# A fused attention and mixer kernel: the last batch's up products by seven products of quarters, joined score chunks for pairs 4 to 6, later transposes, key copies on VectorE

## The chip, the cores and the metric

One core of a Trainium2 chip. The metric is the device time of one execution in microseconds (us); less is better. The core has five engines that work side by side: TensorE (PE, with PEld for its weight loads), VectorE (DVE), ScalarE (ACT), GpSimd (POOL) and SyncE (SP, which issues most DMAs here). Each engine runs its own instructions in order and waits on semaphores for the others.

## What is computed

Attention with a local window, global keys and a linear bias, then a mixer: a low-rank product over the tokens and a two-layer product over the channels, each added to its input.

```python
# q, k, v: [4, 8, 768, 64]; n_global = 8, n_local = 96
scores = q @ k.T / 8                       # per batch and head
keep = (pos_k < 8) | ((rel >= 0) & (rel < 96))
a = softmax(where(keep, scores - slope[h] * dist, -1e9))
x = (a @ v).transpose(0, 2, 1, 3).reshape(4, 768, 512)
h = x.transpose(0, 2, 1) @ U @ V           # U: [768, 32], V: [32, 768]
u = x + h.transpose(0, 2, 1)
out = u + maximum(u @ w_ch1, 0) @ w_ch2    # [512, 2048], [2048, 512]
```

`u @ w_ch1` with its maximum is called the up products here, the product with `w_ch2` the down products.

## The kernel before

**Work and its order.** Heads are taken in pairs: 16 pairs, four to a batch (`NP = 4`). The order of all instructions is the order in which the Python code issues them (a manual schedule, L153); no planner moves them. Pairs 0 to 3 run in the loop at L778. Pairs 4 to 15 and two rounds more run in the loop at L835. One round `i` of it does the scores and exponentials of pair `i`, the product with v of pair `i - 1`, the low-rank part of pair `i - 1`, and, between these, a number of units of the channel products of earlier batches: `fill(n)` (L743) issues `n` units, and the tuple at L838 says how many stand at each place. `unit()` (L757) takes an up unit from `ups_q` or a down unit from `downs_q`, in turn as long as both are there and an up group is less than two groups ahead. `queue_ff(b)` (L604) puts the units of batch `b` into the queues; it is called for batch 3 in round 17. What is left after the loop runs at L937.

**Scores.** A pair's scores have 1408 columns for each of two heads (`W`), in three chunks of 512, 512 and 384. `scores` (L348) issues a chunk's matmuls (64 rows of the array each, one head in each half). Chunks 0 and 1 go to the two banks of the tile "sc" (one buffer, L82), and so does chunk 2 in `st_S(i, 2)`. `s_dve` (L401) then lets VectorE scale a chunk, add the bias and write it to the tile "sp" (one buffer). In `st_S12` (L422), used for pairs 7 to 15 (`joined`, L866), chunk 2 follows chunk 1 at once and goes to two of the three "th" banks (L90); VectorE reads chunk 2 first and chunk 1 later. `st_E` (L428) is the exponential on ScalarE, one instruction per head. `st_V` (L435) is the product with v, into the bank "ob" (one buffer).

**Transposes.** For pairs 1 to 7 `st_T` (L243) turns q and k by twelve transposes on TensorE into two "th" banks; ScalarE copies q out (L276), VectorE k (L277). `st_KA` (L287) makes a copy of the keys in which the global keys stand at the head of each block: two copies, on GpSimd for pairs 5 to 7 (L280). Pairs 8 to 15 are transposed by DMA.

**Up units.** A group is 256 tokens, three groups to a batch. An up unit (`mk_up`, L643) is eight matmuls with 256 columns (tokens) into one "th" bank, the weights `w1_16` in place, and one Relu of ScalarE that empties the bank into `htr` (L658):

```python
for k in range(2):
    jt = 2 * jp + k
    for dc in range(done, NDC):
        nc.tensor.matmul(hps[:, k * FT:(k + 1) * FT],
                         w1_16[:, dc, jt * P:(jt + 1) * P], uT[:, dc, ts], ...)
```

Eight units make a group. `uT` is the transposed `u`; the part of each pair comes by a DMA transpose (`st_X`, L520).

**Down units.** For batches 1 to 3 the down products of a group are done by seven products of quarters (`mk_product`, L697; a form of Strassen's method by Winograd): x1, y1, x2, y2, x3, y3, x4, eight matmuls with 256 columns each into one of two banks; after each, VectorE adds the bank to `x_sb` (L712). Their sums of weights (t1 to t4) are made once, their sums of `htr` (s1 to s4) per group by VectorE (`queue_sums`, L622; `queue_sum`, L568), each issued at the place in the order where `fill` takes it from the queue.

Of the kernel before, what the change touches and what calls it, by code (L numbers as in the profile page):

```python
# [11 lines left out]
FP32 = mybir.dt.float32  # L12
FP16 = mybir.dt.float16
# [3 lines left out]
ALU = mybir.AluOpType  # L17
# [3 lines left out]
def kernel(  # L21
# [44 lines left out]
    HJ = NJC // 2  # L66
    HD = DM // 2
    WG = tuple((b, g) for b in range(1, B) for g in range(NFG))

    cst = ctx.enter_context(tc.tile_pool(name="cst", bufs=1))  # L70
    wbig = ctx.enter_context(tc.tile_pool(name="wbig", bufs=1))
# [8 lines left out]
    def ps_sc():  # L80

        return psum.tile([P, 2, 512], FP32, name="sc", tag="sc", bufs=1)  # L82
# [160 lines left out]
    def st_T(i):  # L243
        stq, stk = cast.pop(i)
        qT = kp.tile([P, S], FP16, name="qT", tag="qT")
        kT = kp.tile([P, S], FP16, name="kT", tag="kT")
        kA = kp.tile([P, NSB - 1, P], FP16, name="kA", tag="kA")
        tps = []
        for st in (stq, stk):

            tp = ps_th("tp", FP16, S)
            tps.append(tp.rearrange("d (n p) -> d p n", n=NSB))
            for n in range(NSB):
                nc.tensor.matmul(  # L254
                    tp[:, n * P:(n + 1) * P], st[:, n].rearrange("s h d -> s (h d)"), ident16,
                    is_transpose=True, start=(n == 0), stop=(n == NSB - 1),
                )
# [161 lines left out]
    def st_S(i, c):  # L419
        s_dve(i, scores(i, c, False))  # L420
# [178 lines left out]
    def weight(w, j):  # L599
        return tw[w][:, j] if w != "t3" else tw[w][j // 2][:, j % 2]  # L600

    first_ups = []

    def queue_ff(b):  # L604
        for g in range(NFG):
            queue_group(b, g)
        if b == 0:
            for c in range(4):
                for made in first_ups:
                    ups_q.extend(made[2 * c:2 * c + 2])  # L610

    def queue_group(b, g):
# [101 lines left out]
                    store(*what)  # L714
            return go

        if b:
            for at in range(NJC // 2):
                ups_q.append((mk_up(at), (b, g)))
        else:  # L720
            first_ups.append([(mk_up(at), (b, g)) for at in range(NJC // 2)])
# [10 lines left out]
        else:  # L732
# [2 lines left out]
                order.sort(key=lambda u: max(1, u[1]))  # L735
            for u in order:
                downs_q.append((mk_down(*u), (b, g)))

    ahead, held, kept = [0], [True], deque()

# [94 lines left out]
    for i in range(NP, NPAIR + 2):  # L835
# [139 lines left out]
```

## Time and profile before

| what | value |
|---|---|
| median of 3 runs | 228.5 us (228.26 to 228.91) |
| the profiled execution | 227.39 us |
| its span, first to last instruction | 225.6 us |
| busy: TensorE / weight loads / VectorE / ScalarE / GpSimd | 218.0 / 171.4 / 156.1 / 126.2 / 73.8 us |
| granted TensorE clock | 1.000 |
| up matmuls (L653) | 756, 95.0 us busy |
| down matmuls of products (L707) | 504 |

The page of the profile gives busy times per engine, the span in 40 slices (each digit a busy share in tenths), the chain of work that ended last (followed back from the last instruction to what released it, step by step), and groups of equal instructions. A group's row reads: line, engine, operation, output<-input, shapes, count | busy us, mean ns of one | idle us just before them and what ended it. A row of the timeline reads: start us, length us, engine, line, operation, shapes, count, and in brackets the idle time before and what ended it. Matmuls overlap in the array: a matmul's recorded length is longer than the distance to the next one's start, and only starts tell the rate.

### The profile page before, as it was taken

To read this page: it belongs to the slowest core of one execution; us is meant where nothing else is said; L and a number is where in the kernel's file an instruction comes from. 1 tells how busy PE (TensorE), PEld (TensorE's weight loads), DVE (VectorE), ACT (ScalarE), POOL (GpSimd) and SP (SyncE) were. 2 spreads that over 40 slices of the span, in tenths; PEclk is the share of its full clock that TensorE was granted. 3 is DMA by queue.
4 is the path that set the end of the run, shared out by engine and by line. 5 is a ranking of instruction groups with operands and counts; after the bars stand their busy time and mean duration, and the time that the engine had idled before them with its cause. 6 is when DMAs were issued, how large, how long until landed. Compare 5 with 4: busy or idle time off the path is not lost.

```text
span 225.6 us, 5876 instructions
## 1 busy us (share of the span) xinstructions
PE 218.0 (97%) x2420; PEld 171.4 (76%) x2420; DVE 156.1 (69%) x320; ACT 126.2 (56%) x197; POOL 73.8 (33%) x124
## 2 busy tenths in 40 slices
PE   7989999999999999999999999999999999999993
PEld 2456678788754547888888888888998888888882
DVE  3798665749488988598989698898575534435552
ACT  6777867685806254967584947473733433333320
POOL 6498828297547412231313132313111000000000
PEclk9999999999999999999999999999999999999999
DMA  6999999969998999998989994960622102020112
GB/s 193 316 287 257 283 219 238 324 120 172 195 169 177 195 230 232 209 255 200 195 224 220 252 229 116 140 170 12 102 59 77 53 1 96 0 93 3 46 49 94
DMA packets 86563, 36.68 MB, mean 163 GB/s; under 512 B 74152, under 2 KB 83592, under 8 KB 86536
## 3 DMA queue, kind: packets, MB, share of 16 engines
q1 hardware_dynamic: 81480, 32.01, 60.6%
q0 software_dynamic: 5056, 4.29, 12.7%
q8 instruction: 19, 0.31, 0.6%
q14 instruction: 8, 0.07, 0.1%
HBM read 27.46 MB, written 6.29 MB: 150 GB/s over the span
## 4 chain that ended last, share of the span: by engine, by line
PE 85%; DVE 8%; ACT 2%; DMA 2%; issue 0%; SPq 0%
PE hps L653 35%; PE cx L707 13%; PE cy L707 10%; PE cps L688 9%; PE sc L367 3%; PE tp L254 3%; PE ob L448 2%; PE ob L444 2%; PE sc L533 2%; DMA kst<-in_k_dram 2%; PE sc L374 2%; ACT ep L431 1%; DVE x_sb L467 1%; DVE sp L413 1%; DVE x_sb L712 1%; DVE kA L290 1%
## 5 line engine op out<-in xcount | busy, mean ns | idle before, releaser
L653 PE MATMUL hps<-uT,w 128*128 128x256 f16 x756 | 95.0, 273 | 0.0
L658 ACT ACTIVATE htr<-hps 128x512 f16<-128x512 f32 x96 | 56.6, 600 | 55.7 <-PE hps L653 55.7
L653 PEld LDWEIGHTS <-w 128*128 128x128 f16 x756 | 71.2, 98 | 9.1
L413 DVE SCALAR_TENSOR_TENSOR sp<-sc,relcat 128x1024 f32<-128x1024 f32 (+1 forms) x27 | 32.1, 1189 | 8.5 <-PE sc L374 4.1
L431 ACT ACTIVATE ep<-sp 128x1408 f16<-128x1408 f32 x24 | 33.2, 1384 | 0.0
L470 POOL CAST x<-x_sb 128x384 f16<-128x384 f32 x27 | 14.2, 527 | 48.3 <-DVE x_sb L467 44.8
L707 PEld LDWEIGHTS <-htr 128*128 128x128 f16 x288 | 27.2, 98 | 3.1
L712 DVE TENSOR_TENSOR x_sb<-cx,x_sb 128x256 f32<-128x256 f32 x36 | 15.2, 421 | 19.0 <-PE cx L707 18.3
L688 PE MATMUL cps<-w,htr 128*128 128x512 f16 x96 | 23.9, 379 | 0.0
L707 PEld LDWEIGHTS <-s 128*128 128x128 f16 x216 | 20.4, 98 | 2.7
L541 POOL CAST x<-x_sb 128x768 f16<-128x768 f32 x12 | 10.2, 851 | 31.2 <-DVE x_sb L538 31.2
L712 DVE TENSOR_TENSOR x_sb<-cy,x_sb 128x256 f32<-128x256 f32 x27 | 11.4, 422 | 12.6 <-PE cy L707 12.4
L467 DVE TENSOR_TENSOR x_sb<-ob,rcp 128x384 f32<-128x384 f32 x30 | 16.7, 558 | 1.1
L367 PEld LDWEIGHTS <-kT 64*128 64x128 f16 x192 | 8.6, 93 | 11.5 <-issue 10.1
L448 PE MATMUL ob<-v,ep 128*128 128x65 f16 x192 | 16.4, 194 | 0.0
L367 PE MATMUL sc<-qT,kT 64*128 64x128 f16 x192 | 15.7, 220 | 0.0
L448 PEld LDWEIGHTS <-ep 128*128 128x128 f16 x192 | 13.8, 98 | 2.0 <-issue 0.3
L688 PEld LDWEIGHTS <-htr 128*128 128x128 f16 x96 | 8.4, 98 | 8.3
L444 PE MATMUL ob<-vA,ep 128*128 128x65 f16 x160 | 14.3, 194 | 0.2 <-DVE vA L317 0.2
L142 POOL CAST v<-vst 128x768 f16<-128x768 f32 x16 | 13.5, 842 | 3.0 <-DMA vst<-in_v_dram 3.0
L538 DVE TENSOR_TENSOR x_sb<-sc,x_sb 128x768 f32<-128x768 f32 x12 | 11.5, 958 | 4.0 <-PE sc L533 3.9
L374 PE MATMUL sc<-qT,kA 64*128 64x128 f16 x160 | 13.3, 217 | 0.8 <-DVE kA L290 0.6
(111 smaller groups left out, 319.2 us busy)
## 6 DMA issues: line engine op xcount, KB each, us to landing
qst<-in_q_dram SPq DMA_DIRECT2D x16, 384.0 KB, 4.0
kst<-in_k_dram SPq DMA_DIRECT2D x16, 384.0 KB, 5.7
vst<-in_v_dram SPq DMA_DIRECT2D x16, 384.0 KB, 4.0
out_dram<-x_sb SPq DMA_DIRECT2D x23, 256.0 KB, 2.0
w<-in_moe_w_ch_dram POOLq DMA_DIRECT2D x8, 512.0 KB, 8.1
vA<-v SPq DMA_DIRECT2D x8, 152.3 KB, 3.3
out_dram<-x_sb SPq DMA_DIRECT2D x2, 128.0 KB
uT<-x SPq DMA_TRANSPOSE x12, 4.4
```

The lines of the kernel that those rows point to most:

```text
L367: nc.tensor.matmul(scs[hi][:, o:o + P], kT[r, kb * P:(kb + 1) * P], qT[r, kb * P:(kb + 1) * P], start=(o == 0 and not on_pe), stop=(o + P ...
L374: nc.tensor.matmul(scs[hi][:, o + P:o + 2 * P], kA[r, kb], qT[r, (kb + 1) * P:(kb + 2) * P], start=False, stop=(o + 2 * P == tot),)
L413: nc.vector.scalar_tensor_tensor(out=sps[i][:, :, c0:c0 + tot], in0=both[:, :, 0:tot], scalar=qk_scale / slope[2 * (i % NP)], in1=relfs[c0 ...
L431: nc.scalar.activation(eps[i][:, hi], sps[i][:, hi], AF.Exp, scale=slope[2 * (i % NP)])
L444: nc.tensor.matmul(ob[:, qi], ep[:, OF[qi - 1]:OF[qi - 1] + P], vA[:, qi - 1, hi], start=True, stop=False,)
L448: nc.tensor.matmul(ob[:, qi], ep[:, DG[qi]:DG[qi] + P], vt[:, qi, hi], start=(qi == 0), stop=True,)
L467: nc.vector.tensor_tensor(xo, ob[:, :, 0:D], rb, ALU.mult)
L653: nc.tensor.matmul(hps[:, k * FT:(k + 1) * FT], w1_16[:, dc, jt * P:(jt + 1) * P], uT[:, dc, ts], start=(dc == 0 and k == 0), stop=(dc == ...
L658: nc.scalar.activation(cell["htr"][:, 2 * jp:2 * jp + 2].rearrange("p j t -> p (j t)"), hps, AF.Relu)
L688: nc.tensor.matmul(cps, htr[:, jc, t * P:(t + 1) * P], w2_16[:, jc], start=(b > 0 and jc == 0), stop=(jc == NJC - 1),)
L707: nc.tensor.matmul(ps, cell[a][:, j], weight(w, j), start=(first and j == 0), stop=(done is not None and j == HJ - 1), skip_group_check=True,)
L712: nc.vector.tensor_tensor(x_sb[:, n, cs], ps, x_sb[:, n, cs], ALU.add)
```

## The change

- **Up products of batch 3.** The 24 up units are replaced by seven products of quarters for each group and each of two halves of the hidden channels (`st`): 42 steps of eight matmuls with 128 columns. The four tiles of weight sums per half (`up_sums`) are made by VectorE from round 15 on, in buffers that the loads of q and k and "sp" no longer need. Four token differences per group (`token_sums`) are made by VectorE between the rows. Products 1, 6, 7 and 4 pile up in one "th" bank, 5 and 3 in a bank of "sc", 2 in "ob". ScalarE copies the banks after 2, 3 and 5 to SBUF; VectorE adds those copies to the "th" bank after 1, 6 and 7 and writes `htr`; ScalarE applies the Relu, in place for these, from the bank for 4. Two or three steps make a row, which takes the place of an up unit in `ups_q`; the steps of a group's end are mixed with the first of the next.
- **Pairs 4 to 6** use `st_S12`, as pairs 7 to 15 do.
- **The transposes of pairs 5 to 7** (`st_T(i + 1)`) move from behind `st_V(i - 1, 0)` to the place where chunk 2 of pairs 4 to 6 was; the load of the last quarter of `w1` now is issued on GpSimd's queue ahead of them instead of behind.
- **The key copies of pairs 5 to 7** go to VectorE.

```diff
         if i > NP:
-            st_KA(i, nc.gpsimd)
+            st_KA(i, nc.vector)
@@
+    def up_sums():
+        made = {0: [], 1: []}
+        room = scp.tile([P, 2 * W], FP32, name="uw", tag="sp", bufs=1)
+        later_set = room[:, 0:16 * P].bitcast(FP16).rearrange("p (x d n) -> p x d n", x=4, d=2)
+        part["p2"] = room[:, 16 * P:20 * P]
+        for st in range(2):
+            js = [slice(h * DFF // 2 + st * 4 * P, h * DFF // 2 + (st + 1) * 4 * P) for h in range(2)]
+            w = {f"a{h + 1}{d + 1}": w1_16[:, 2 * d:2 * d + 2, js[h]] for h in range(2) for d in range(2)}
...
+            for name, a, b_, op in (
+                ("s1", "a21", "a22", ALU.add), ("s2", "s1", "a11", ALU.subtract),
+                ("s4", "a12", "s2", ALU.subtract), ("s3", "a11", "a21", ALU.subtract),
+            ):
+                made[st].append((f"tw{name}", st, w[name], w[a], w[b_], op))
+    def queue_up_sums(st):
+        if st == 0:
+            uw["sums"] = up_sums()
+        for k, x in enumerate(uw["sums"][st][0:3 if st else 4]):
+            queue_sum(*x, wait=k)
+    def token_sums(g, t):
...
+        return [(f"tu{g}{n}", 0, q_[n], q_[a], q_[b_], ALU.subtract) for n, a, b_ in (
+            ("t1", "b12", "b11"), ("t2", "b22", "t1"), ("t3", "b22", "b12"), ("t4", "b21", "t2")
+        )]
+    def queue_products(b, cells, sums):
+        yy = ps_sc()
...
+        def add(g, st, h, t, x, y):
+            to = out_of(g, st, h, t)
+            x, y = (z.rearrange("p (j t) -> p j t", j=4) for z in (x, y))
+            nc.vector.tensor_tensor(to, x, y, ALU.add)
+            nc.scalar.activation(to, to, AF.Relu)
+        def step(g, st, k):
...
+            bank, a, t = {
+                1: ("x", "a11", "b11"), 2: ("z", "a12", "b21"), 3: ("y", "s4", "b22"),
+                4: ("x", "a22", "t4"), 5: ("y", "s1", "t1"), 6: ("x", "s2", "t2"),
+                7: ("x", "s3", "t3"),
+            }[k]
...
+            for j in range(4):
+                for dc in range(2):
+                    nc.tensor.matmul(
+                        ps[:, j * P:(j + 1) * P], uw[st][a][:, dc, j * P:(j + 1) * P],
+                        turns[g][t][:, dc], start=(k in (1, 2, 5) and j == 0 and dc == 0),
+                        stop=(k in (2, 3, 4) and j == 3 and dc == 1), skip_group_check=True,
+                    )
+            early = g == WU[0][1] and st == 0
+            if k in (2, 3, 5):
...
+                nc.scalar.copy(part["p5", st] if k == 5 else part[f"p{k}"], ps)
+            if k == 1:
+                add(g, st, 0, 0, ps, part["p2"])
+            elif k == (3 if early else 6):
+                add(g, st, 0, 1, made[at, "x"], part["p3"])
+            elif k == 7:
+                add(g, st, 1, 1, ps, part["p5", st])
+            elif k == 4:
+                nc.scalar.activation(
+                    out_of(g, st, 1, 0), ps.rearrange("p (j t) -> p j t", j=4), AF.Relu
+                )
+                sums[g](st)
+        rows = []
+        for _, g in WU:
+            first = g == WU[0][1]
+            if first:
+                rows += [[(g, 0, 2), (g, 0, 1)], [(g, 0, 5), (g, 0, 6)], [(g, 0, 3), (g, 1, 5)]]
+            else:
+                rows[-2].insert(0, (g, 0, 5))
+                rows[-1].insert(0, (g, 0, 2))
+                rows += [[(g, 0, 1), (g, 0, 3)], [(g, 0, 6), (g, 1, 5)]]
+            rows += [[(g, 1, 2), (g, 0, 7)], [(g, 1, 1), (g, 0, 4)], [(g, 1, 3), (g, 1, 6)],
+                     [(g, 1, 7)], [(g, 1, 4)]]
+        between = {k: uw["sums"][1][x:x + 1] for k, x in ((4, 3),)}
+        for k, (_, g) in enumerate(WU):
+            for at, x in ((7 * k - 2, (0, 1)), (7 * k, (2,)), (7 * k + 1, (3,))):
+                if k == 0:
+                    at += 2
+                between.setdefault(at, []).extend(todo[g][y] for y in x)
...
@@ the loop over pairs 4 to 15
         if i == NP:
             load_w1(2)
-        if i + 1 < NPE:
-            st_T(i + 1)
-        if i == NP:
             load_w1(3)
         fill(next(units))
-        joined = live and i >= NPE - 1
-        if joined:
+        if live:
             mid = st_S12(i)
-        elif live:
-            st_S(i, 1)
         fill(next(units), quiet=i > NP + 1 and (i - 2) % NP == NP - 1)
         if NP < i <= NPAIR:
             st_V(i - 1, 1)
-        if joined:
+        if live:
             s_dve(i, mid)
...
         fill(next(units))
-        if live and not joined:
-            st_S(i, 2)
+        if i + 1 < NPE:
+            st_T(i + 1)
         fill(next(units))
...
+        if NPAIR - 1 <= i:
+            queue_up_sums(i - NPAIR + 1)
```

A row's entry is (group, half, product); `between` names the rows after which VectorE makes token differences.

More of the change, by code (lines that the diff above doesn't have):

```diff
@@ L68 @@
     WG = tuple((b, g) for b in range(1, B) for g in range(NFG))
+    WU = tuple((B - 1, g) for g in range(NFG))
     cst = ctx.enter_context(tc.tile_pool(name="cst", bufs=1))
@@ new lines, in queue_products, with out_of, mk_row, go @@
+    def queue_products(b, cells, sums):
+        yy = ps_sc()
+        made = {}
+        rooms = [scp.tile([P, W], FP32, name="tu", tag="ep") for _ in range(2)]
+        places = [rooms[g // 2][:, g % 2 * 4 * P:(g % 2 + 1) * 4 * P] for g in range(NFG)]
+        part["p3"] = rooms[1][:, 4 * P:8 * P]
+        todo = {
+            g: token_sums(g, places[g].bitcast(FP16).rearrange("p (x d n) -> p x d n", x=4, d=2))
+            for _, g in WU
+        }
+        def out_of(g, st, h, t):
+            return cells[g]["htr"][:, h * HJ + 4 * st:h * HJ + 4 * st + 4, t * P:(t + 1) * P]
+        def add(g, st, h, t, x, y):
[4 more added lines that the diff above has]
+        def step(g, st, k):
+            at = (g, st)
+            if "htr" not in cells[g]:
+                cells[g]["htr"] = ffp.tile([P, NJC, FT], FP16, name="htr", tag="htr", bufs=3)
+            if k == 1:
+                made[at, "x"] = ps_th("hps")
+            elif k == 2:
+                made[at, "z"] = ps_ob()
+            elif k == 5:
+                made[at, "y"] = yy[:, st]
+            bank, a, t = {
[3 more added lines that the diff above has]
+            }[k]
+            if a[0] == "s":
+                need((f"tw{a}", st))
+            if t[0] == "t":
+                need((f"tu{g}{t}", 0))
+            ps = made[at, bank]
+            for j in range(4):
[7 more added lines that the diff above has]
+            if k in (2, 3, 5):
+                if k == 5:
+                    part["p5", st] = stp.tile([P, 4 * P], FP32, name="p5", tag="vst", bufs=2)
+                nc.scalar.copy(part["p5", st] if k == 5 else part[f"p{k}"], ps)
+            if k == 1:
+                add(g, st, 0, 0, ps, part["p2"])
[13 more added lines that the diff above has]
+                rows += [[(g, 0, 2), (g, 0, 1)], [(g, 0, 5), (g, 0, 6)], [(g, 0, 3), (g, 1, 5)]]
+            else:
+                rows[-2].insert(0, (g, 0, 5))
[9 more added lines that the diff above has]
+                between.setdefault(at, []).extend(todo[g][y] for y in x)
+        def mk_row(n):
+            def go():
+                for s_ in rows[n]:
+                    step(*s_)
+                for x in between.pop(n, ()):
+                    nc.vector.tensor_tensor(*x[2:])
+                    have.add(x[:2])
+            return go
+        for n, row in enumerate(rows):
+            ups_q.append((mk_row(n), (b, row[-1][0])))
@@ L602 @@
     first_ups = []
     def queue_ff(b):
+        cells, sums = {}, {}
         for g in range(NFG):
-            queue_group(b, g)
+            cells[g], sums[g] = queue_group(b, g)
+        if (b, 0) in WU:
+            queue_products(b, cells, sums)
         if b == 0:
@@ L715, in mk_product @@
             return go
-        if b:
+        if (b, g) in WU:
+            pass
+        elif b:
             for at in range(NJC // 2):
```

15 lines of the change are left out of this document (added).

## Prediction

> **What bounds the kernel now.** I read the page's busy times first, then its slices, then the chain of work that ended last.
>
> ```profile
> PE 218.0 (97%) x2420; PEld 171.4 (76%) x2420; DVE 156.1 (69%) x320; ACT 126.2 (56%) x197; POOL 73.8 (33%) x124
> ...
> PE   7989999999999999999999999999999999999993
> ...
> DVE  3798665749488988598989698898575534435552
> ACT  6777867685806254967584947473733433333320
> POOL 6498828297547412231313132313111000000000
> ```
>
> TensorE (PE) is full from the third slice on. The other engines matter only where TensorE waits for them. The chain says the same: 85% of the span is TensorE, 35% of it the up products.
>
> ```profile
> PE 85%; DVE 8%; ACT 2%; DMA 2%; issue 0%; SPq 0%
> ```
>
> Two stretches are touched. The first is 31 to 60 us (pairs 4 to 6). There is one pair of it below, in the timeline of TensorE (start, length, line):
>
> ```profile
> 39.79 0.23 PE L367 MATMUL sc<-qT,kT 64*128 64x128 f16 x2
> ...
> 40.47 0.50 PE L254 MATMUL tp<-ident,q 128*128 128x128 f16 x6
> 41.05 0.49 PE L254 MATMUL tp<-ident,k 128*128 128x128 f16 x6
> 41.53 1.03 PE L653 MATMUL hps<-uT,w 128*128 128x256 f16 x8
> 42.50 0.23 PE L367 MATMUL sc<-qT,kT 64*128 64x128 f16 x2
> ```
>
> Lengths include a pipeline tail of 0.17 us; starts count. Eight 256-wide matmuls from 41.53 last 0.873 (0.109 each, as everywhere), so they end at 42.40. The scores begin 0.10 later, and leaving the scores costs another 0.09 (last start 55.26 plus 0.06, next matmul 55.41). That is the price of each visit to the scores. The k transposes should have begun at 40.47 + 6 x 0.056 = 40.81 and began 0.24 late, the next unit 0.14 late: both waited for ScalarE to empty one of the three "th" banks behind two Exps, as ScalarE's timeline shows:
>
> ```profile
> 39.12 1.39 ACT L431 ACTIVATE ep<-sp 128x1408 f16<-128x1408 f32 x1
> 40.39 1.09 ACT L658 ACTIVATE htr<-hps 128x512 f16<-128x512 f32 x2
> ```
>
> (The second Relu ends at 41.48, TensorE starts at 41.53: 0.05 from release to matmul.)
>
> The second stretch is the last batch's up products, from 177.09 to the end of TensorE at 221.63. Busy time by window:
>
> ```profile
> 187.00:200.00 13.00, 13.00 (x121) 11.66 (x120) 5.59 (x13) 4.69 (x9) 0.00 (x0) 1.00 0.11 42
> ```
>
> TensorE has no gap; VectorE (third number) is at 5.6 of 13, ScalarE at 4.7, the granted clock is 1.00. The durations that I use are these (last numbers: busy, mean ns), with the latency from the timeline: a product ends at 190.19, VectorE's add starts at 190.39, so 0.20.
>
> ```profile
> L658 ACT ACTIVATE htr<-hps 128x512 f16<-128x512 f32 x96 | 56.6, 600 | 55.7 <-PE hps L653 55.7
> ...
> L693 DVE TENSOR_TENSOR x_sb<-cps,x_sb 128x512 f32<-128x512 f32 x6 | 4.1, 681 | 0.0
> ```
>
> ```profile
> 190.39 0.42 DVE L712 TENSOR_TENSOR x_sb<-cx,x_sb 128x256 f32<-128x256 f32 x1 [2.19 <-PE cx L707]
> 190.73 0.41 DVE L571 TENSOR_TENSOR s<-htr 128x512 f16<-128x512 f16 x1
> ```
>
> ```profile
> 69.99 0.49 PE L533 MATMUL sc<-tmp,v16w 128*128 128x128 f16 x6
> 70.33 0.38 PE L688 MATMUL cps<-w,htr 128*128 128x512 f16 x1
> ```
>
> The next VectorE instruction starts 0.08 before the last one's end (190.39, 190.73), when it depends on nothing; on ScalarE it is 0.12. Six 128-wide matmuls take 0.34: 0.056 each, their weight loads included.
>
> **The change, part by part.**
>
> **1. Products.** Out go 24 units of 8 matmuls, 192 x 0.1092 = 20.97. In come 42 steps (7 products, 2 halves, 3 groups) of 8 matmuls of 128 columns: 336 x 0.056 = 18.82. Gain 2.15 on TensorE. The trace has such matmuls only in runs of 6 to 12; here they come in runs of 8 to 24, each with a new weight. The weight-load row is 98 ns long, but 65-wide matmuls with a load each start every 0.031 (11 in 0.35, from 40.12), so loads keep up. The Trainium skill speaks against this: "TensorE: Matmul & The Clock Gate", section "Back-to-back issue gap", gives about 81 ns per matmul for a sustained stream of 128 columns with weight loads. By it the 336 would take 27.2 and lose 6.2 where I count a gain of 2.15; the row of 0.056 differs from it, in short runs.
>
> **2. What the products add on VectorE and ScalarE.** Per group: six adds of a bank and a stored part (512 wide, float32 in: 0.68, from L693), four token differences (256 wide, half words: 0.29, between L271's 0.17 for 24 columns and L571's 0.42 for 512), eight copies or Relus from PSUM and six Relus in place (0.60 each, from L658 and L391's 0.594). VectorE rises from 5.6 to 5.6 + 6 x 0.68 + 4 x 0.29 = 10.8 of about 12.4, ScalarE to 14 x 0.60 = 8.4. Neither is the bound by sum. But TensorE must now wait for adds inside a chain: products 1, 6, 7 and 4 pile up in one bank, and VectorE reads it between them. A step is 0.448, a down product 0.874. I went through the instruction order with these figures:
> - *Handing over to the next group* (3 times, the start included). Step 3 and then step 6 end; a down product (0.87) follows; then step 5 of the next group needs t1. The copy of step 3's bank ends 0.20 + 0.60 after step 3, which is 0.35 after step 6; the add of step 6 waits for it and starts at 0.39; VectorE takes t1 behind it at 0.99; t1 is there at 0.99 + 0.29 + 0.05 = 1.33. TensorE comes at 0.87 and waits **0.46**. Three times 1.38.
> - *The double row* between groups 0 and 1, the only place without a down product between: step 7, step 2 (0.45), step 4. Counted from step 6's end again, VectorE does t1, t2, s1, the add of the down product, s2, and begins the add of step 7 at 2.43; it is through at 3.11 + 0.05, TensorE is there at 2.67: **0.49**.
> - *The last two rows* hold one step each. Step 7 comes 0.87 after step 6 but its bank is free at 0.39 + 0.68 + 0.05 = 1.12: **0.25**; step 4 likewise waits behind two sums and an add: **0.29**.
> - Elsewhere the slack is positive, least 0.16 (step 1 to step 6: 1.32 between them; the add needs 0.20 + 0.22 of queue + 0.68 + 0.05).
>
> Sum of waits 2.41, less 2.15: the tail **loses 0.26**. The add's bounds are the rows 0.43 (L571, half words) and 0.96 (L538, 768 wide): with 0.43 the waits sum to 0.88 (tail -1.27), with 0.96 to 5.7 (+3.6). I take 0.68, whose width and types are nearest. t1 at 0.17 or 0.42 moves the tail by -0.37 or +0.64.
>
> **3. Eight weight sums** (1024 wide, half words, about 0.75: the t rows of L571) go to VectorE from 160 to 186 us. There it idles 1.6 before 162.44 and 2.2 before 177.29; the longest delay is 0.4 at 162.44, on a bank that TensorE wants 1.7 later. Nothing.
>
> **4. Joined chunks, pairs 4 to 6.** One visit to the scores less per pair: 3 x 0.19 = **-0.57**. The waits of 0.24 and 0.14 above go too: **-0.38**, since transposes no longer stand behind two Exps. Late next:
> - *The "sc" banks.* Between chunk 0 and chunk 1 there stood a pair's V (0.35), transposes (0.67) and a unit (0.87). Now only V and the unit: 0.09 + 0.35 + 0.87 + 0.10 = 1.41, and VectorE needs 0.20 + 1.22 (L413) + 0.05 = 1.47: **0.07** in pair 6. In pair 5 L413 starts 0.30 later still, behind the Exp that empties the single "sp" buffer (trace of before: 40.54 where 40.23 was possible): **0.38**.
> - *The "th" banks.* Chunk 2 takes two of three. The unit after the joined visit needs the bank of the unit before: 0.60 later, where Relu needs 0.20 + 0.60 + 0.05 = 0.85: **0.18** in pair 6 (0.25 less its 0.07), none in pair 5, which waited already. In pair 4 the third bank is held by a unit begun earlier, so the next unit waits for chunk 2's first read: 0.20 + 0.55 (L407) + 0.05, less the 0.31 that TensorE has: **0.50**.
>
> **5. Transposes later, pairs 5 to 7.** They take two banks right behind a unit; the unit after them needs that unit's bank 0.67 later, not 0.85: **0.19** x 3 = 0.57. The 0.41 before the first of them (31.22) stays: the first unit waits for the same copy.
>
> **6. Key copies.** 0.72 + 0.21 leave GpSimd; about 0.33 + 0.17 (from L267's 0.26 for 384 columns, and L271) join VectorE, behind a copy after which it idles (0.97 before 47.34). Nothing; without that cover 0.5 a pair. The weight load moved ahead of the transposes on GpSimd's queue is issued some 5 us earlier; its first reader is several units away. Nothing; SP's queue keeps its order.
>
> Parts 4 and 5: 0.45 + 0.68 + 0.57 - 0.57 - 0.38 = **+0.75**. Whole: 0.26 + 0.75 = **+1.0**. The profiled run took 227.39 (span 225.6 and 1.8 around it), so it would take 228.4. The median of before is 228.5, 1.1 above that run; I add the same 1.0: **229.5**.
>
> **Rivals.**
> - *Faster:* VectorE's queue, in the hand-over of the last batch. If t1 comes within 0.87 of step 6 instead of 1.33 (copy, add and difference together 0.46 shorter), the three waits go, with it most of the others, and the 2.15 stay: 228.5 - 2.15 + 0.75 = 227.1. For it: VectorE has a slack of 1.6 per group. Against it: the order, in which t1 stands behind an add that waits for a copy.
> - *No change:* the adds run at the half-word row's 0.43: tail -1.27, all -0.5: 228.0.
> - *VectorE becomes the bound:* adds near 0.8 to 0.96 (two float32 inputs, an output with strides): tail +1.2 to +3.6, 230.4 to 232.8, middle 231.5. For it: VectorE is at 87%.
> - *Weight loads pace the long runs:* 336 x 0.098 - 20.97 = +12.0 if nothing of a load is hidden, 241.5 with part 4 and 5. Against it: the 0.056 and 0.031 above. By the page's 81 ns it would be 235.5.
>
> **How the numbers follow.** 0.3% is 0.7 us, about what a measurement of this kernel can tell from no change. Forecast 0.54 (0.45 of it beyond +0.7, 0.09 within); faster rival 0.13; no change 0.20; VectorE bound 0.09; weight loads 0.04. So faster 0.13, same 0.29, slower 0.58. The range goes from 227.3 to 231.3; it leaves out the weight loads, most of the VectorE rival's upper end and half of the faster rival.
>
> **What would show it.** Timeline of the tail: 128-wide starts 0.056 apart (else part 1 fails); gaps of about 0.46 before step 5's first matmul, ended by VectorE's difference; one of 0.49 in the double row; adds of 0.68. In 31 to 60 us: TensorE idle about 0.5 after the first joined visit, 0.2 after each transpose pair. If the tail has no gaps over 0.1, part 2 is wrong and the kernel is faster; if the units after transposes start at once, part 5 is.

## The result, and the profile after

The kernel after takes 230.61 us (median of 6 runs, 230.30 to 231.13), the kernel before 228.38 beside it (227.8 to 227.9 in the larger sets of runs below). The ratio is **1.0123, 95% interval [1.0099, 1.0146]**: slower, by about 2.8 us where 1.0 was forecast. (The two medians alone are 2.2 apart, a quotient of 1.0098; the ratio on record agrees with the 227.8 of the larger sets.) The profiled execution took 230.86 us with a span of 229.1, against 227.39 and 225.6.

The page of after, its busy times, its slices of TensorE (PE) and VectorE (DVE), and its chain:

```profile
PE 217.8 (95%) x2562; PEld 172.3 (75%) x2564; DVE 177.2 (77%) x367; ACT 136.1 (59%) x215; POOL 71.6 (31%) x118
...
PE   7889989999999999999999999999999898999993
...
DVE  3688765768598988598798797798996776877772
...
PE 72%; DVE 12%; ACT 7%; DMA 3%; issue 2%; SPq 1%; POOL 1%; DVEq 0%; ACTq 0%
```

TensorE's recorded busy time is all but the same in a span 3.5 us longer: its idle time went from 7.6 to 11.3 us. Two slices near the end, full before, have become 8, the chain's share of TensorE has fallen from 85% to 72%, and ScalarE (ACT), 2% before, has 7%. TensorE's waits in after, by the instruction that waits and the one that it waits for (us in total, times, longest), name the places:

```profile
PE sc L690 <- ACT tu L699: 1.4, 3, 0.7
...
PE sc L690 <- DVE tu L736: 1.0, 3, 0.3
...
PE hps L690 <- DVE htr L665: 0.4, 1, 0.4
PE hps L797 <- DVE sp L408: 0.3, 1, 0.3
...
PE sc L368 <- DVE sp L414: 0.3, 1, 0.3
```

The second, third, fourth and fifth are waits that the prediction named: three hand-overs, the double row, the unit after the first joined visit, the "sc" banks of pair 5. The first, the largest, it did not have. (This view counts idle time after the modelled end of the last matmul; by starts, as the prediction counts, each wait is 0.17 longer.)

To tell where time went I cut each span in four: up to the last low-rank product of pair 3 (code that the change doesn't touch), from there to the first 512-wide down product (pairs 4 to 6), from there to TensorE's end (in which the last batch's products lie), and 3.95 behind it in every kernel. The first stretch differs from execution to execution of the same code, the other two hardly do.

| us | first stretch | pairs 4 to 6 | to TensorE's end | span |
|---|---|---|---|---|
| before | 31.22 | 28.24 | 162.17 | 225.58 |
| after | 31.70 | 28.79 | 164.64 | 229.09 |

So the change costs **0.55 in pairs 4 to 6 and 2.47 in the products**, 3.0 together; the other 0.48 between the two profiles lies in the first stretch, whose code is the same. The prediction had 0.75 and 0.26. Three of the profiles read below (early differences, key copies alone, load alone) are of slow executions, whose first stretch was late by 4.3 to 6.5 us; only their later stretches are read.

What it took for durations held. Three groups of after, the matmuls of product 5 and two of the adds (last numbers before the idle part: busy, mean ns):

```profile
L690 PE MATMUL sc<-tu,uw 128*128 128x128 f16 x48 | 3.7, 219 | 2.4 <-ACT tu L699 1.4 <-DVE tu L736 1.0
...
L665 DVE TENSOR_TENSOR htr<-hps,tu 128x512 f16<-128x512 f32 x6 | 4.1, 688 | 2.3 <-ACT tu L699 2.3
L665 DVE TENSOR_TENSOR htr<-hps,p 128x512 f16<-128x512 f32 x6 | 4.1, 687 | 1.3 <-PE hps L690 1.3
```

The adds take 0.688 (0.68 was taken). The starts of 128-wide matmuls that follow one another are 0.056 apart (median of the 294 pairs inside the steps), also in the runs of 16 and in the one of 32, with a new weight each. The 2.15 of TensorE's gain is there. What ate it is seen in the timeline of after, around the first of the long waits:

```profile
180.51 0.61 PE L690 MATMUL sc<-tu,uw 128*128 128x128 f16 x8 [0.33 <-DVE tu L736]
...
182.27 0.61 PE L690 MATMUL sc<-uT,uw 128*128 128x128 f16 x8
...
182.92 0.59 ACT L699 COPY tu<-sc 128x512 f32<-128x512 f32 x1 [1.13 <-PE sc L690]
183.54 0.69 DVE L665 TENSOR_TENSOR htr<-hps,tu 128x512 f16<-128x512 f32 x1 [0.55 <-ACT tu L699]
183.56 0.61 PE L690 MATMUL sc<-tu,uw 128*128 128x128 f16 x8 [0.67 <-ACT tu L699]
```

The first line is the hand-over's wait, as predicted. The second is product 3 of the first half, by starts through at 182.72. The fifth is the step behind it in the same row, product 5 of the second half. It goes to the other bank, and its operands have long been there. Yet it starts only when ScalarE's copy of product 3's bank ends (182.92 + 0.59 = 183.51, 0.05 later the matmul): 0.84 by starts. The two banks are one tile, `yy = ps_sc()`, of which the half `st` gets `yy[:, st]`, and a write to one half waits for the reader of the other. It comes in every group: 0.84, 0.53 and 0.53 us, 1.90 in all.

### The profile page after: what moved, and what is told of

It is laid out like the page before. It is cut to its first block, busy times and chain, and to the rows that moved or that the text cites. A ratio compares the mean times of both kernels' runs of the same rounds, so it can differ in the third digit from the quotient of the medians.

```text
span 229.1 us, 6251 instructions
## 1 busy us (share of the span) xinstructions
PE 217.8 (95%) x2562; PEld 172.3 (75%) x2564; DVE 177.2 (77%) x367; ACT 136.1 (59%) x215; POOL 71.6 (31%) x118
## 4 chain that ended last, share of the span: by engine, by line
PE 72%; DVE 12%; ACT 7%; DMA 3%; issue 2%; SPq 1%; POOL 1%; DVEq 0%; ACTq 0%
PE hps L797 24%; PE cx L851 11%; PE cps L832 9%; PE cy L851 7%; DVE htr L665 4%; DMA vst<-in_v_dram 3%; PE sc L368 3%; PE ob L449 2%; PE tp L255 2%; PE sc L534 2%; PE ob L445 2%; PE hps L690 2%; ACT htr L666 2%; DVE sp L414 2%; PE sc L375 2%
## 5 line engine op out<-in xcount | busy, mean ns | idle before, releaser
L797 PE MATMUL hps<-uT,w 128*128 128x256 f16 x564 | 70.7, 273 | 0.6 <-DVE sp L408 0.3
L802 ACT ACTIVATE htr<-hps 128x512 f16<-128x512 f32 x72 | 42.3, 601 | 34.9 <-PE hps L797 34.8
L797 PEld LDWEIGHTS <-w 128*128 128x128 f16 x564 | 52.7, 98 | 7.8 <-issue 0.9
L414 DVE SCALAR_TENSOR_TENSOR sp<-sc,relcat 128x1024 f32<-128x1024 f32 x24 | 29.2, 1217 | 6.9 <-PE sc L375 4.2
L851 PEld LDWEIGHTS <-htr 128*128 128x128 f16 x288 | 26.7, 98 | 2.9
L666 ACT ACTIVATE htr<-htr 128x512 f16<-128x512 f16 x18 | 11.3, 630 | 14.8 <-DVE htr L665 14.8
L856 DVE TENSOR_TENSOR x_sb<-cy,x_sb 128x256 f32<-128x256 f32 x27 | 11.3, 419 | 4.9 <-PE cy L851 4.7
L690 PEld LDWEIGHTS <-uw 128*128 128x128 f16 x192 | 11.7, 98 | 4.0 <-issue 2.6
L832 PEld LDWEIGHTS <-htr 128*128 128x128 f16 x96 | 8.4, 97 | 8.3
```

The costliest lines, as they stand in the source:

```text
L414: nc.vector.scalar_tensor_tensor(out=sps[i][:, :, c0:c0 + tot], in0=both[:, :, 0:tot], scalar=qk_scale / slope[2 * (i % NP)], in1=relfs[c0 ...
L690: nc.tensor.matmul(ps[:, j * P:(j + 1) * P], uw[st][a][:, dc, j * P:(j + 1) * P], turns[g][t][:, dc], start=(k in (1, 2, 5) and j == 0 and ...
L797: nc.tensor.matmul(hps[:, k * FT:(k + 1) * FT], w1_16[:, dc, jt * P:(jt + 1) * P], uT[:, dc, ts], start=(dc == 0 and k == 0), stop=(dc == ...
L802: nc.scalar.activation(cell["htr"][:, 2 * jp:2 * jp + 2].rearrange("p j t -> p (j t)"), hps, AF.Relu)
L832: nc.tensor.matmul(cps, htr[:, jc, t * P:(t + 1) * P], w2_16[:, jc], start=(b > 0 and jc == 0), stop=(jc == NJC - 1),)
L851: nc.tensor.matmul(ps, cell[a][:, j], weight(w, j), start=(first and j == 0), stop=(done is not None and j == HJ - 1), skip_group_check=True,)
```

## The experiments

The times of the kernel before in these sets are 227.77 to 227.94 (medians of 21 to 29 runs).

**The split bank.** The whole change; the second half's product 5 (and 3) gets a bank of its own.

```diff
-                made[at, "y"] = yy[:, st]
+                made[at, "y"] = yy[:, 0] if st == 0 else ps_th("yps")
```

> The changed kernel, with the bank of products 5 and 3 of the second half taken from the 'th' banks, so that the two halves no longer share the two-bank tile 'sc'. Nothing else differs. Theory A (the account of the prediction holds, but product 5 of the second half also waits for the copy of product 3 of the first half, because both lie in one tile): the three waits of 0.84, 0.53 and 0.53 us in the profile after go away, 1.9 in all, and the waits of 0.50 (three times), 0.57, 0.30 and 0.28 stay: about 228.7 where the changed kernel took 230.6, 1.001 to 1.005 of the kernel before. Rival B (VectorE and ScalarE, at 10 of 13 us, are the bound, and the shared tile only shows where TensorE meets them): the waits move to other steps, 230.2 or more, 1.008 or more of before.

Products 162.71, 1.93 less than after; pairs 4 to 6 28.80, as after. The timeline of this kernel at the same place:

```profile
182.29 0.61 PE L690 MATMUL sc<-uT,uw 128*128 128x128 f16 x8
182.74 0.61 PE L690 MATMUL yps<-tu,uw 128*128 128x128 f16 x8
182.94 0.59 ACT L699 COPY tu<-sc 128x512 f32<-128x512 f32 x1 [1.13 <-PE sc L690]
183.19 1.04 PE L851 MATMUL cy<-t,s 128*128 128x256 f16 x8
183.56 0.69 DVE L665 TENSOR_TENSOR htr<-hps,tu 128x512 f16<-128x512 f32 x1 [0.55 <-ACT tu L699]
```

Product 5 now starts 0.45 behind product 3, the copy runs beside it, and the down product has begun before the copy ends. The three waits are gone, every other one stays (0.50 three times, 0.59, 0.30, 0.28). In time it is 229.95, ratio 1.0080 [1.0053, 1.0107]: slower than the 1.0048 that its stretches add up to, and by time alone in the rival's range. But no wait moved to another step, which the rival needs, so the waits' cause is settled and what else the timed runs cost is not; further profiles below bear on it.

**The products alone**, with the scores, transposes and key copies of before.

> The kernel before with the seven products of the last batch alone; pairs 4 to 6, their transposes and key copies as before. Theory A: the stretch from 31 to 60 us costs 0.55 to 0.75 us in the changed kernel, so this one takes 229.9 to 230.1, about 1.007 to 1.009 of before. Rival (the joined chunks pay for themselves): 230.6 or more.

Pairs 4 to 6 28.24, products 164.64, the very stretch of after; 230.13, ratio 1.0094 [1.0061, 1.0126]. In the stretches the two halves of the change don't touch each other: 2.47 us are the products'.

**The products alone with the split bank** (the edit of the first experiment made to the second).

> Only the products of the change (scores, transposes, key copies as before), with product 5 of the later half in a bank of its own. Against the run with the products only (1.0094) this has one edit. Theory (the whole tile's wait is the term that the prediction lacked): products 0.54 us over the up units of before (2.65 of waits less 2.15 and what is small), nothing else: ratio 1.001 to 1.004. Rival (in timed runs something else of the products costs): ratio 1.005 or more.

Products 162.73, 0.56 over before; 228.22, ratio **1.0014 [0.9987, 1.0042]**. In time, too, one tile's layout decides: 1.0094 with it, 1.0014 without.

**Pairs 4 to 6 alone** (joined chunks, late transposes, earlier load, key copies on VectorE; the up units of before).

> The kernel before with the joined chunks, the later transposes and the key copies on VectorE alone; up products of the last batch as before. Theory A: waits of 0.50, 0.38, 0.18 and three of 0.19 on the 'th' and 'sc' banks outweigh 0.57 for fewer visits and 0.38 of old waits: 228.9 to 229.2, 1.002 to 1.004 of before. Rival (visits saved and nothing lost): 227.4 to 227.8, 0.996 of before.

230.30, ratio 1.0095 [1.0058, 1.0132]: three times what was expected. The stretch is 30.04, 1.80 over before, of which 0.55 are the waits of after and 1.25 is one wait that after's profile doesn't have. The timeline of this kernel there (POOL is GpSimd):

```profile
48.79 0.33 DVE L295 COPY kA<-kT 128x640 f16<-128x640 f16 x1
48.85 1.48 POOL L231 DMA_DIRECT2D w<-in_moe_w_ch_dram  x2
...
49.15 0.72 DVE L296 COPY kA<-kT 128x32 f16<-128x32 f16 x1
...
49.78 1.53 DVE L318 COPY vA<-v 8x520 f16<-8x520 f16 x1
50.31 0.84 POOL L124 CAST q<-qst 128x768 f16<-128x768 f32 x1
...
51.24 0.27 DVE L498 CAST tmp<-ob 128x128 f16<-128x128 f32 x1
...
51.56 0.49 PE L534 MATMUL sc<-tmp,v16w 128*128 128x128 f16 x6 [1.09 <-DVE tmp L498]
```

and the same place in after:

```profile
47.50 1.52 POOL L231 DMA_DIRECT2D w<-in_moe_w_ch_dram  x2
47.80 0.73 DVE L296 COPY kA<-kT 128x32 f16<-128x32 f16 x1
...
48.44 0.28 DVE L318 COPY vA<-v 8x520 f16<-8x520 f16 x1
48.64 0.27 DVE L498 CAST tmp<-ob 128x128 f16<-128x128 f32 x1
...
49.02 0.84 POOL L124 CAST q<-qst 128x768 f16<-128x768 f32 x1
```

A copy of 32 columns, 0.17 in the other two pairs, takes 0.72 beside GpSimd's weight loads. The one behind it (8 x 520) takes 0.28 in after; here it lasts until GpSimd has issued its second load and made its cast of q (50.31 + 0.84 = 51.15, the copy ends at 51.31). Behind it in VectorE's queue is the cast that TensorE needs. The page "SBUF — State Buffer" of the Trainium skill, section "SBUF: two separate sides", says that GpSimd and VectorE, in VectorE's faster modes or with two inputs from SBUF, share a pair of ports as a lock that whoever starts first keeps for a whole instruction. The trace agrees in part. VectorE's copy isn't slowed in proportion, it ends only when GpSimd is through. But here it stayed held through the cast, which GpSimd began 0.53 after the copy's recorded start, and in after it took its 0.28 although it began, as here, 0.20 behind GpSimd's second load; there that load took 0.79, here 0.75. What decides between the two isn't seen.

**Key copies back on GpSimd**, in the whole change.

```diff
-            st_KA(i, nc.vector)
+            st_KA(i, nc.gpsimd)
```

> The kernel after with one edit: the key copies of pairs 5 to 7 go back to GpSimd. Theory (a copy of half words on VectorE that meets GpSimd at work is held until GpSimd is through, as in the run with the middle alone, where the copy behind the key copies took 1.53 us in place of 0.28 and TensorE waited 1.25): no such wait near 50 us; in the profile the middle as after (0.55 over before, +-0.2), in the timed runs 0.3 to 0.7 us less than after, ratio 1.009 to 1.011. Rival (the hold was an accident of that one run, the key copies cost nothing on either engine): ratio as after, 1.011 to 1.014.

Stretches 28.79 and 164.71, as after; 231.59, ratio 1.0135 [1.0092, 1.0179]. No gain: the first expectation failed in time, and the ratio lies in the rival's range. After's own profile has no held copy, and its timed runs (230.30 to 231.13) leave little room for one. With the key copies on GpSimd the 8 x 520 copy on VectorE still takes 0.77, beside GpSimd's copy of 640 columns, in this profile and in the four others with that order; TensorE waits for it in none of them.

**Pairs 4 to 6 alone, key copies on GpSimd.**

> Joined chunks, late transposes and the earlier weight load, without the products and with the key copies on GpSimd as before. Theory (the run with the middle alone was slower than its waits because VectorE's copies were held): stretch of pairs 4 to 6 +0.5 to +0.6 us, ratio 1.002 to 1.004, less than the middle with the key copies (1.0095). Rival (the excess comes from something else that the middle does, the earlier weight load or the joining): ratio 1.007 to 1.011.

Stretch 28.79 (+0.55); 228.49, ratio **1.0012 [0.9986, 1.0038]**, where the same with the key copies on VectorE had 1.0095. The joined chunks, the late transposes and the earlier load cost 0.55; by this pair of runs the rest of that run's loss was the key copies.

**Key copies on VectorE alone**, the rest as before.

> The kernel before with one edit: the key copies of pairs 5 to 7 on VectorE. Prediction (part 6): nothing, stretch within 0.1, ratio 0.999 to 1.001. Theory of the held copies: GpSimd loses 0.93 a pair and issues the weight loads and casts earlier, VectorE's copies meet them; in the profile one key copy or the copy of v's global rows behind it takes 0.7 us or more in place of 0.17 or 0.28, and in some executions TensorE waits up to 1.3 us; ratio 1.001 to 1.005 with a wider spread.

Stretch 29.18 (+0.94); 229.49, ratio 1.0065 [1.0040, 1.0090]. In this stretch no copy was held; the sign expected in the trace was wrong, the loss wasn't. The timeline of this kernel in pair 4, VectorE with TensorE's next scores:

```profile
40.03 0.33 DVE L294 COPY kA<-kT 128x640 f16<-128x640 f16 x1
40.39 0.17 DVE L295 COPY kA<-kT 128x32 f16<-128x32 f16 x1
40.47 1.22 DVE L413 SCALAR_TENSOR_TENSOR sp<-sc,relcat 128x1024 f32<-128x1024 f32 x1
41.74 0.23 PE L367 MATMUL sc<-qT,kT 64*128 64x128 f16 x2
```

In before that scaling starts right behind the copy of k (0.88 after it began); here 1.44 after, and chunk 2 waits 0.20 more for the "sc" bank. Pair 5 loses 0.05 so, pair 6 0.20, and in pairs 5 and 6 the low-rank steps behind are 0.11 and 0.12 late each. In the changed order of after the scaling isn't behind the key copies, and these waits are not there.

**The whole change with the split bank, key copies on GpSimd**, and then four more profiled executions, timed once each: two of this kernel, two of that with the key copies on VectorE (the first experiment's).

> The whole change with the split bank and with the key copies of pairs 5 to 7 on GpSimd. Against the run with the split bank alone (1.008) this has one edit. Theory A (the stretches of the traces add up: 0.54 of products and 0.55 of pairs 4 to 6): ratio 1.003 to 1.006, and the run with the split bank was above it for the key copies that VectorE's queue holds in some executions. Rival (the two halves of the change cost more together than apart): ratio 1.007 to 1.010, as with the key copies on VectorE.

> A second look at the whole change with the split bank. Theory (the excess is chance in code that the change doesn't touch): the stretches of pairs 4 to 6 and of the products are 0.55 and 0.54 over before within 0.1, and what the run takes more lies before pair 4 or in single waits for a DMA. Rival (the change itself costs it): the same wait of 0.5 or more shows inside pairs 4 to 6 or among the products in most of the four looks.

> A third look at the same kernel. Theory: 0.55 and 0.54 over before within 0.1, the rest before pair 4 or in single waits for a DMA. Rival: a wait of 0.5 or more inside pairs 4 to 6 or among the products, as in the second look.

> A second look at the whole change with the split bank and the key copies on GpSimd. Theory (the wait of 2.0 for uT was one late DMA): no such wait, 0.55 and 0.3 to 0.55 over before, the rest before pair 4. Rival (the joined chunks move the issue of that DMA so that it is late often): the wait shows again, 0.3 or more.

> A third look at the same kernel. Theory: no wait for uT, 0.55 and 0.3 to 0.55 over before, the rest before pair 4. Rival: the wait for uT shows again, 0.3 or more.

All six profiles of the two kernels, by the engine of the key copies:

| us | first stretch | pairs 4 to 6 | to TensorE's end | span |
|---|---|---|---|---|
| VectorE, first | 31.73 | 28.80 | 162.71 | 227.19 |
| VectorE, second | 32.66 | 30.04 | 163.51 | 230.16 |
| VectorE, third | 31.16 | 30.04 | 162.76 | 227.92 |
| GpSimd, first | 32.12 | 28.79 | 164.56 | 229.42 |
| GpSimd, second | 31.05 | 28.79 | 162.75 | 226.53 |
| GpSimd, third | 31.79 | 28.79 | 162.76 | 227.29 |

Both new profiles with VectorE's key copies show the held copy, 1.25 us at the same instruction. Of the profiles with VectorE's copies in this order it is 3 in 5 (after and the split bank's first without, pairs 4 to 6 alone and these two with it), of those with GpSimd's none in 5. So the rival was right for VectorE: in some executions the change itself costs it. How much of the time that is isn't settled. If three in five held for the split bank, 0.54 + 0.56 + 0.75 = 1.85 us, ratio 1.008, would be what its runs measured; but the same kernel with GpSimd's copies, where no profile has that wait, measured 1.0076, and the whole change without the split bank 1.0123 with VectorE's copies and 1.0135 with GpSimd's. In time, only pairs 4 to 6 alone and the key copies alone show what the copies cost.

The stretch of 164.56 in the first profile with GpSimd's copies holds another wait, seen in its timeline:

```profile
134.29 0.49 PE L797 MATMUL hps<-uT,w 128*128 128x256 f16 x3
136.73 0.70 PE L797 MATMUL hps<-uT,w 128*128 128x256 f16 x5 [1.96 <-DMA uT<-x]
```

An up unit stood 2.0 us for the transposing DMA of `uT`. The second profile with VectorE's copies has 0.9 at the same kind of place. It lies in code that the change leaves alone, and the two later profiles of the same kernel don't have it; but two of the six profiles of the whole change with the split bank show it and none of the other 13, so whether the change makes it likelier is open. The ratio with GpSimd's copies, 1.0076 [1.0044, 1.0109], is above the 1.005 of its stretches without that wait and in the range of the rival (the two halves cost more together than apart: 1.0014 and 1.0012 apart). Whether such late DMAs make up all of that isn't settled.

**The joining alone** (`joined = live`, the rest as before).

> The kernel before with joined chunks for pairs 4 to 6 alone; transposes at their old place, key copies on GpSimd. Theory A (the three 'th' banks set the price): the transposes hold two banks, so chunk 2 must wait until VectorE has copied k, 0.6 to 0.75 in each of three pairs, and the unit after the first joined visit waits 0.5: about +2.0 us, 230.2 to 230.6, 1.008 to 1.010 of before. Rival (a visit saved is 0.19 gained): 227.8, 0.9975 of before.

Stretch 29.73 (+1.49, less than the 2.0 expected); 229.23, ratio 1.0053 [1.0025, 1.0082]. Without the late transposes the joining costs more than both together: chunk 2 now waits 0.43 to 0.46 inside each of the three visits, and the unit after it 0.45 for a "th" bank in pair 4. So the late transposes aren't only a cost; they make room for the joining.

**The late transposes alone.**

> The kernel before with one edit: the transposes of pairs 5 to 7 move behind chunk 2 of the pair (which stays a visit of its own). Theory (part 4 of the prediction: without the transposes between them, chunk 1 comes before VectorE has read chunk 0 out of its banks): the old waits of 0.24 and 0.16 in pair 5 go, 0.38 (pair 5) and 0.14 (pair 6) come before chunk 1, and no wait after the transposes, since chunk 2 stands between them and the unit whose bank they need; stretch +0.0 to +0.2 us, ratio 1.000 to 1.001. Rival (the late transposes cost 0.18 by themselves wherever they stand): +0.5 to +0.7, ratio 1.002 to 1.003.

Stretch 28.32 (+0.08); 227.72, ratio 0.9995 [0.9966, 1.0023]. The waits came where the prediction's part 4 puts them: 0.38 before pair 5's chunk 1 and 0.13 in pair 6, with the old 0.24 and 0.16 gone. The 0.18 after the transposes isn't there, since chunk 2 stands between.

**The earlier load alone** (`load_w1(3)` ahead of the transposes).

> The kernel before with one edit: the load of the last quarter of w1 is issued on GpSimd's queue ahead of the transposes and their key copies. Prediction (part 6): nothing, stretch within 0.1 us, ratio 0.999 to 1.001. Rival (the load issued early takes DMA time from the loads of q and k or stands on GpSimd's queue ahead of a copy that TensorE waits for): stretch +0.3 or more, ratio 1.002 to 1.005.

Stretch 28.24 and products 162.13, exactly before; but 229.33, ratio 1.0053 [1.0023, 1.0083]. In its profile the loss lies at 23 us, in a wait of 2.8 us for the cast of k, before the moved load is issued; the profiles of the early differences and of the key copies alone have the same wait, 2.8 and 3.2 us, and their kernels don't move the load. The stretches say nothing, the times say 0.5%: what its other executions did isn't known, and this stays open.

**Early differences.** The split bank, before's scores, transposes and key copies, and t1 and t2 of each group made two rows earlier (the first group's ahead of its first row, by three more lines).

```diff
-            for at, x in ((7 * k - 2, (0, 1)), (7 * k, (2,)), (7 * k + 1, (3,))):
+            for at, x in ((7 * k - 4 if k else -3, (0, 1)), (7 * k, (2,)), (7 * k + 1, (3,))):
...
```

> Scores, transposes and key copies as before. The products as after, with two edits: the later half's product 5 has a bank of its own, and the first two token differences of a group (t1, t2) are made by VectorE two rows earlier (the first group's before its first row). Theory (the tail's extra time is waits, the products themselves gain): the three waits of the whole tile go, as with the bank apart (-1.9), and the three waits of 0.5 at the hand-over to the next group go too (-1.5). Left are about 0.6 in the double row and 0.3 + 0.3 in the last two rows, against a gain of 2.15: the products end 0.9 to 1.1 us sooner than the up units of before, ratio 0.995 to 0.997. Rival (VectorE is the bound; the order only decides where its lateness shows): the waits come back in other rows, products stretch not shorter than before, ratio 0.999 to 1.004.

Products 161.48, 0.69 less than before where 0.9 to 1.1 was expected; 227.22, ratio **0.9970 [0.9943, 0.9998]**. The three waits at the hand-over are gone, the double row has 0.71 and the last rows 0.30 and 0.28. VectorE is no bound: outside the double row TensorE runs 13 of 13 us, as it did before the change, with VectorE at 10.2. Such a window of this kernel among its products (length, then busy us of PE, PEld, DVE, ACT, POOL, the granted clock):

```profile
203.00:216.00 13.00, 13.00 (x183) 12.36 (x181) 10.20 (x24) 8.28 (x15) 0.00 (x0) 1.00 0.11 42
```

against a window of after among the same products (not the same rows to the us), where VectorE has hardly more to do and TensorE waits:

```profile
203.00:216.00 13.00, 12.30 (x167) 11.33 (x165) 10.58 (x25) 7.71 (x14) 0.00 (x0) 1.00 0.11 42
```

**Rows laid anew**, on top of that.

```diff
-                rows += [[(g, 0, 2), (g, 0, 1)], [(g, 0, 5), (g, 0, 6)], [(g, 0, 3), (g, 1, 5)]]
+                rows += [[(g, 0, 2), (g, 0, 1), (g, 0, 5)], [(g, 0, 6), (g, 0, 3), (g, 1, 5)]]
...
+            if g == WU[-1][1]:
+                rows += [[(g, 1, 2), (g, 0, 7)], [(g, 1, 1), (g, 1, 3)], [(g, 1, 6), (g, 0, 4)],
+                         [(g, 1, 7)], [(g, 1, 4)]]
+                continue
...
-            for at, x in ((7 * k - 2, (0, 1)), (7 * k, (2,)), (7 * k + 1, (3,))):
+            for at, x in ((7 * k - 5, (0, 1)), (7 * k - 1, (2,)), (7 * k, (3,))):
...
```

> As the run with the split bank and early differences, with the rows laid out anew: the first group's first six steps in two rows of three in place of three rows of two, so that a down product is left for the place between the two rows that had none; and in the last group product 3 of the later half a row earlier, product 6 in the row of product 4 of the earlier half. Theory (what is left of the waits is order, not VectorE's load): the 0.71 of the double row and one of the 0.3 of the last rows go, products 1.5 to 1.7 us shorter than the up units of before, ratio 0.992 to 0.994. Rival (VectorE is now so full that a wait only moves): products within 0.3 of the run with early differences (0.7 shorter than before), ratio 0.996 to 0.998.

Products 161.24, 0.93 less than before, not 1.5 to 1.7; 227.42, ratio **0.9963 [0.9936, 0.9989]**. The 0.71 and one 0.3 went, but the denser first rows got waits of 0.32 and 0.30, and product 7 at the end of the first group one of 0.24. Both expectations were half right. This and the kernel before it are the two that beat before.

## Why the prediction was wrong

- **Direction and three of its parts right, size wrong.** Slower by 2.8 in time, 3.0 by the stretches, for a forecast of 1.0.
- **The step that failed** is in part 2, "Elsewhere the slack is positive, least 0.16". A slack at product 5 of the second half is there only if the two banks are free of each other, as product 5 and product 3 write different ones (the prediction doesn't say that it took them so); the program has them as one tile, and TensorE waited 0.84, 0.53 and 0.53 there. The split bank takes exactly these out (1.93), and the products alone fall from 1.0094 to 1.0014 with it. The diff shows the tile: `yy = ps_sc()` and `yy[:, st]`. The wait stands in the program, at product 5 of the half 1, for ScalarE's copy of product 3 of the half 0. The products lost 2.47 for a forecast of 0.26: 1.90 by this step, 0.24 more in the waits that were named, 0.17 in part 3, less 0.10 that I can't place.
- **Part 1 right.** 0.056 a matmul, 2.15 gained. The weight-load rival fell with it, and so did the Trainium skill's 81 ns for a stream of 128 columns ("TensorE: Matmul & The Clock Gate", "Back-to-back issue gap"): the median of 294 pairs here is 56 ns, in runs of 8, 16 and once 32 matmuls (the prediction had 8 to 24).
- **Part 2's named waits right.** Hand-overs 0.50, 0.50, 0.50 (predicted 0.46), double row 0.57 (0.49), last rows 0.30 and 0.28 (0.25 and 0.29): 2.65 for 2.41. The latencies, the durations and the order on VectorE were close to those predicted.
- **Part 3 wrong by 0.17.** The product with v of pair 15 starts at 165.13, 0.17 late, behind three weight sums of VectorE. One of them took 1.19 in place of 0.68, starting beside GpSimd's cast of x (161.55 to 162.38).
- **Parts 4 and 5 right in mechanism, 0.2 too dear.** Waits measured (predicted): 0.48 (0.50) before 33.62, 0.18 three times (0.19), 0.38 (0.38) in pair 5, 0.14 and 0.11 (0.07 and 0.18) in pair 6. Their sum less 0.57 and the old 0.40 is 0.68, the stretch gives 0.55; 0.13 I can't place. The timeline of after:

```profile
33.62 1.91 PE L797 MATMUL hps<-uT,w 128*128 128x256 f16 x16 [0.32 <-DVE sp L408]
...
42.70 0.23 PE L368 MATMUL sc<-qT,kT 64*128 64x128 f16 x2 [0.31 <-DVE sp L414]
```

- **Part 6 wrong, though not in after's own profile.** "Nothing" was true only where the copy behind the key copies wasn't held. In three of five profiled executions it was, for 1.25 us; in before's order the same move costs 0.94, a wait at each place behind. In the timed runs of the whole change the engine of the key copies makes no difference that can be seen, so this isn't the step that made the forecast too small. The prediction had looked for cover on VectorE (idle time after the copies) and not at what GpSimd does at that moment. Of the earlier load only the stretch is known to be unchanged.
- **The rivals.** VectorE as the bound would have given 230.4 to 232.8, and 230.6 was measured, by another mechanism: adds 0.688 and not 0.8 to 0.96, and in the longest wait VectorE stands idle 0.55 (the row at 183.54). The "faster" rival, t1 early enough, is what the early differences do; they gain 1.2 over the split bank, as its 1.5 less the longer double row would have it. The weight-load rival's 241.5 should be 241.2 (228.5 + 12.0 + 0.75), which changes nothing.

## What to carry to other kernels

In this program a wait was for the whole tile of two banks and not for the bank: before counting on two banks to overlap, look whether they are one tile, and give each a tile of its own if one is read while the other is written. When a chain of products is made to share an engine's result inside the chain, lay out that engine's queue in order, not its sum: here 10.2 us of 13 were enough with one order and too late with another. Work moved from GpSimd to VectorE needs a look at what GpSimd runs at that moment, not only at VectorE's idle time.

## What the runs showed that was not expected

- A copy of half words on VectorE can be held by what GpSimd runs: one of 0.28 took 1.53 in three profiled executions of five. The starts of the two engines' instructions just before it, measured from GpSimd's first load, differ by less than 0.01 us between the held executions and the others, so the traces don't show what decides.
- Single executions vary by as much as the change does: the first stretch, the same code throughout, took 31.05 to 33.05 in 16 profiles, a held copy is 1.25, a late DMA 0.9 or 2.0. A difference of 0.3 to 0.5% in 6 to 12 runs of this kernel is no proof by itself (the earlier load: 1.0053 with unchanged stretches). The stretches of the traces behind the first agree within 0.1 from execution to execution where no such wait falls in them.
